# Query projection in bursts of eight heads with paired 64-row TensorE tiles, and shared staging for the output product, in a fused attention-and-MLP kernel

## The chip, the cores and the metric

The kernel runs on one core of a Trainium2 chip. The metric is the device time of one execution in microseconds (us), lower is better. Times are medians of several runs. A single-core run is called fast when it lies within 1.5% of the fastest of the same kernel, and slow otherwise. Kernels are compared only within the same rounds. Engines: PE is the tensor engine (PEld its weight loads), DVE the vector engine, ACT the scalar engine, POOL is GpSimd and SP the engine that issues most transfers.

## The reference

Shapes: 2048 tokens, model width D = 576, 32 query heads over 16 key/value heads of 128, of which the last W = 512 cached positions are used; MLP width 4608. Everything is bf16.

```python
def A(xn, k_cache, v_cache, wq, wo):          # attention, 32 heads
    q = split_heads(xn @ wq)                  # 576 -> 32 x 128
    scores = q @ k^T * 128 ** -0.5            # last 512 positions
    return merge_heads(softmax(scores) @ v) @ wo

def B(xn, w1, w2, w3, w4):
    h = gelu(layernorm(xn) @ w1)
    hs = shift_four_quarters(h) @ w2          # +1, -1, +2, -2 tokens
    x1 = xn + hs
    return x1 + gelu(layernorm(x1) @ w3) @ w4

xn = layernorm(x)
out = x + A(xn) * silu(B(xn))
```

## The kernel before

The attention stage works through four blocks of 512 tokens, 32 heads each; u = 0 to 127 counts the heads. For each head PE does five q matmuls (576 rows padded to 640), four score matmuls and four groups of value matmuls; ACT takes one exponential per score matmul.

```python
qT_pool = pool("qT_pool", 3)
pT_pool = pool("pT_pool", 10)
o_pool = pool("o_pool", 4)
so_pool = pool("so_pool", 1)                  # staging of the wo product
oT_pool = pool("oT_pool", 36)
ps_sc = pool("ps_sc", 3, PSUM)                # score banks
ps_pq = pool("ps_pq", 2, PSUM)                # q banks, also gelu and MLP parts
ps_po = pool("ps_po", 2, PSUM)                # value banks
ps_wo = pool("ps_wo", 1, PSUM)

def stage_q(u):                               # q of ONE head
    psq = ps_pq.tile([P, QB], FP32, name="psq", tag="pq")
    for kc in range(NDC):                     # 5 x 128 rows, the last half zeros
        nc.tensor.matmul(psq, lhsT=w[:, kc, hh*Dh:(hh+1)*Dh], rhs=xT_b[qb % 2][:, kc, :], ...)
    qT = qT_pool.tile([P, QB], BF16, name="qT")
    copy(out=qT, in_=psq)                     # DVE in block 0, ACT after it

def stage_s(u, kc):                           # one score matmul and its exponential
    sc = ps_sc.tile([P, QB], FP32, name="sc", tag="sc")
    nc.tensor.matmul(sc, lhsT=kT[:, g, kc*P:(kc+1)*P], rhs=qT_t[u], ...)
    pT = pT_pool.tile([P, QB], BF16, name="pT")
    nc.scalar.activation(out=pT, in_=sc, func=Exp, scale=SCALE)

def stage_v(u, t0): ...                       # 8 value matmuls into po, DVE writes o
def stage_t(u):                               # o is transposed by DMA, for wo
    o = o_t.pop(u)
    oT = oT_pool.tile([P, TB, P], BF16, name="oT")
    nc.sync.dma_start(out=oT[:], in_=o[:]..., transpose=True)

for u in ...:
    for i in range(4):
        stage_s(u, i)
        if i == 0:
            stage_q(u + 1)                    # one head ahead
            for fn in fill.get(u, []): fn()   # loads, layer norms: placed BY HEAD NUMBER
            continue
        if i < 3: stage_v(u - 1, 2 * (i - 1))
        for fn in cut[i - 1]: fn()            # wo, gelu, k transposes: BY HEAD NUMBER
    stage_t(u - 1)
# ... cut ...
# MLP: weights load once the last oT transpose is issued
with tc.issue_after(last_t[0].ins):
    for i in range(NSL): load_w(i)
load_sx(0)                                    # reads back what wo wrote to DRAM
load_x1(1)
```

What is not a matmul of the head itself (layer norms, their DMA transposes, the small MLP, the wo product of the block before, all weight loads) is pinned to a head number, at so many heads' distance from what needs it.

## Time and profile before

| | before |
|---|---|
| time, median of the first 3 runs | 850.75 us (850.12 to 870.52) |
| profiled span | 847.5 us |
| PE / ACT / DVE busy | 98% / 54% / 50% |
| PE waits of over 2 us each kind | value groups for DVE 2.0, MLP for a fence 2.1 |
| mean granted PE clock | 0.999 |

The page's row of slices cuts the span into 40 equal slices and gives each engine's busy share in tenths. The stage view gives, per stretch of time, the busy time and the number of instructions of PE, PEld, DVE, ACT and POOL, then the granted clock (1 is full speed), the busy share of the 16 DMA engines and GB/s. The order of time gives start, length, engine, line of the kernel, operation, output<-input; in square brackets stands the idle time just before it and what ended it. The lines of before are shown in the prediction, where they are used.

### The profile page before, as it was taken

The page shows a single profiled execution, that of the slowest core. Times are in us where ns is not written, and L with a number is a line of the kernel's source. Part 1 is how long each engine was busy: PE and PEld are TensorE (multiplying, and loading weights), DVE is VectorE, ACT ScalarE, POOL GpSimd, SP SyncE. Part 2 cuts the span into 40 slices and gives each one's busy share as a digit, 9 for nine tenths or more (in the row PEclk, how much of TensorE's full clock was granted, in tenths as well). Part 3 has the DMA queues.
Part 4 walks back from the last instruction along what each step waited for, and adds up shares of the span by engine and source line. Part 5 has one row for each costly group of instructions (what it writes and reads, how often), then busy time and mean ns, then how long its engine had stood idle before and what let it go on. Part 6 is the DMA issues. An engine that isn't in the chain of part 4 may idle for free.

```text
span 847.5 us, 19375 instructions
## 1 busy us (share of the span) xinstructions
PE 826.8 (98%) x7896; PEld 485.0 (57%) x7980; DVE 427.7 (50%) x1351; ACT 460.9 (54%) x825; POOL 76.9 (9%) x134
## 2 busy tenths in 40 slices
PE   8999899999999999999999999999999999999996
PEld 5665555665564565565566565455555555555555
DVE  5778841267751166762154884052247537635324
ACT  5776763598793388784379874132333333334610
POOL 3441200310010111010001100000000000000000
PEclk9999999999999999999999999999999999999999
DMA  7996751473372174363048336992003301310101
GB/s 181 234 234 159 157 97 41 117 125 91 87 136 43 41 130 99 91 126 82 19 82 164 70 79 105 307 342 47 2 2 74 99 2 43 69 64 15 44 15 46
DMA packets 139983, 83.94 MB, mean 99 GB/s; under 512 B 106944, under 2 KB 133248, under 8 KB 139888
## 3 DMA queue, kind: packets, MB, share of 16 engines
q1 hardware_dynamic: 130048, 53.01, 30.6%
q0 software_dynamic: 8448, 28.15, 11.8%
q10 hardware_dynamic: 1392, 1.48, 0.5%
q8 instruction: 64, 1.05, 0.5%
q14 instruction: 31, 0.25, 0.1%
HBM read 49.17 MB, written 9.44 MB: 69 GB/s over the span
## 4 chain that ended last, share of the span: by engine, by line

## 5 line engine op out<-in xcount | busy, mean ns | idle before, releaser
L367 ACT ACTIVATE pT<-sc 128x512 bf16<-128x512 f32 x512 | 290.3, 596 | 103.5 <-PE sc L365 91.4
L365 PE MATMUL sc<-qT,kT 128*128 128x512 bf16 x493 | 175.1, 378 | 1.3 <-DVE qT L355 0.6
L382 PEld LDWEIGHTS <-pT 128*128 128x128 bf16 x2048 | 139.5, 98 | 52.9 <-DVE o L387 2.5
L382 PE MATMUL po<-v_sb,pT 128*128 128x129 bf16 x2048 | 161.4, 220 | 3.2 <-DVE o L387 2.0
L350 PE MATMUL psq<-xT_b,wq_b 128*128 128x512 bf16 x603 | 151.9, 379 | 2.5 <-DMA xT_b<-xn_b 0.4
L386 DVE RECIPROCAL ri_b<-po 128x2 f32<-128x2 f32 x256 | 43.0, 168 | 189.3 <-PE po L382 185.3
L731 PE MATMUL ph<-xT_b,w_s 64*128 64x512 bf16 x976 | 127.1, 376 | 2.3 <-DVE fence L721 2.1
L768 PE MATMUL pm<-w_s,h 64*128 64x512 bf16 x864 | 122.2, 377 | 0.9 <-DVE fence L721 0.9
L406 PE MATMUL pswo<-wo_sb,oT 128*128 128x512 bf16 x497 | 114.2, 379 | 0.8
L387 DVE TENSOR_TENSOR o<-po,ri_b 128x256 bf16<-128x256 f32 x256 | 107.9, 422 | 10.7 <-DMA oT<-o 4.3
L749 ACT ACTIVATE h<-ph 128x512 bf16<-128x512 f32 x67 | 39.4, 597 | 133.9 <-PE ph L731 133.9
L350 PEld LDWEIGHTS <-wq_b 128*128 128x128 bf16 x640 | 62.4, 98 | 74.4 <-issue 2.2
L768 PEld LDWEIGHTS <-h 64*128 64x128 bf16 x1728 | 70.8, 94 | 56.7 <-issue 1.6
L406 PEld LDWEIGHTS <-oT 128*128 128x128 bf16 x1024 | 64.9, 98 | 55.2
L768 PE MATMUL pr<-w_s,h 64*128 64x64 bf16 x864 | 90.2, 189 | 0.2 <-ACT h L749 0.2
L731 PEld LDWEIGHTS <-w_s 64*128 64x128 bf16 x1152 | 57.3, 94 | 51.0 <-issue 2.8
L357 ACT ACTIVATE qT<-psq 128x512 bf16<-128x512 f32 x96 | 57.4, 598 | 28.1 <-PE psq L350 26.7
L747 DVE COPY hx<-ph 128x512 f32<-128x512 f32 x55 | 38.0, 692 | 67.8 <-PE ph L731 67.8
L365 PEld LDWEIGHTS <-kT 128*128 128x128 bf16 x512 | 47.4, 97 | 28.4 <-DVE qT L355 1.2
L227 POOL DMA_DIRECT2D wq_b<-in_A_wq_dram x30 | 23.4, 780 | 314.4 <-PE psq L350 295.4
L721 DVE TENSOR_SCALAR fence<-ph,ph 1x1 f32<-1x1 f32 x61 | 12.6, 206 | 53.9 <-PE ph L731 53.4
L749 ACT ACTIVATE h<-hx 128x512 bf16<-128x512 f32 x55 | 34.6, 630 | 8.5 <-DVE hx L747 7.0
(114 smaller groups left out, 641.3 us busy)
## 6 DMA issues: line engine op xcount, KB each, us to landing
wq_b<-in_A_wq_dram POOLq DMA_DIRECT2D x30, 512.0 KB, 5.3
w_s<-in_B_w_dram SPq DMA_DIRECT2D x9, 576.0 KB, 7.0
wo_sb<-in_A_wo_dram POOLq DMA_DIRECT2D x8, 576.0 KB, 5.0
w_s<-in_B_w_dram SPq DMA_DIRECT2D x9, 512.0 KB, 7.9
x_dram<-x SPq DMA_DIRECT2D x4, 576.0 KB, 3.5
x<-x_dram SPq DMA_DIRECT2D x4, 576.0 KB, 5.1
s_b<-s_dram SPq DMA_DIRECT2D x4, 576.0 KB, 5.4
x_b<-in_A_x_dram SPq DMA_DIRECT2D x4, 576.0 KB, 6.6
```

The source lines that it names most:

```text
L350: nc.tensor.matmul(psq[:, :], lhsT=w[:, kc, hh * Dh:(hh + 1) * Dh], rhs=xT_b[qb % 2][:, kc, :], start=(kc == 0), stop=(kc == NDC - 1))
L357: nc.scalar.activation(out=qT[:, :], in_=psq[:, :], func=ACT.Copy)
L365: nc.tensor.matmul(sc[:, :], lhsT=kT[:, g, kc * P:(kc + 1) * P], rhs=qT_t[u][:, :], start=True, stop=True)
L367: nc.scalar.activation(out=pT[:, :], in_=sc[:, :], func=ACT.Exp, scale=SCALE)
L382: nc.tensor.matmul(po[:, j, :], lhsT=pTs[kc][:, tt * P:(tt + 1) * P], rhs=v_sb[:, g, kc, 0:Dh + 1], start=(kc == 0), stop=(kc == KCH - 1))
L386: nc.vector.reciprocal(out=ri, in_=po[:, :, Dh])
L387: nc.vector.tensor_tensor(out=o[:, t0:t0 + 2, :], in0=po[:, :, 0:Dh], in1=ri.unsqueeze(2).to_broadcast([P, 2, Dh]), op=ALU.mult)
L406: nc.tensor.matmul(ps, lhsT=oT_t[qb * Hq + h][:, tt, :], rhs=wo_sb[:, h, lo:hi], start=(h == 0), stop=(h == Hq - 1))
L731: nc.tensor.matmul(ps[i][:, :], lhsT=lhsT, rhs=xT[half, kc, :], start=first, stop=last, skip_group_check=True)
L747: nc.vector.tensor_copy(out=src[:, :], in_=ps[i][:, :])
L749: nc.scalar.activation(out=h3[:, :], in_=src[:, :], func=ACT.Gelu_apprx_tanh)
L768: nc.tensor.matmul(out, lhsT=h3_t[b, fc][half, tt * P:(tt + 1) * P], rhs=w4_s[fc // WS][half, fc % WS, lo:hi], start=key not in started, s ...
```

## The change

The intent is to save the zero padding of the q contraction. Two heads share PE as two tiles of 64 rows: both heads' 576 rows are nine half steps each, and two half steps run at once, one in the upper and one in the lower rows. First five pairs (F), then the halves swap banks for four more (S), with a one-element DVE fence between. q is now made for eight heads at a time, in the two q and the two value banks. To make room, the staging of the wo product shares existing buffers, and the o pool goes from 4 to 3.

```diff
-        qT_pool = pool("qT_pool", 3)
+        qT_pool = pool("qT_pool", 8)
-        o_pool = pool("o_pool", 4)
+        o_pool = pool("o_pool", 3)
-        so_pool = pool("so_pool", 1)
...
-            eng.dma_start(out=w[0:DR, NF, :], in_=A_wq[NF * P:D, c0:c0 + 4 * Dh])
+            for half in (LO, HI):
+                eng.dma_start(out=w[half, NF, :], in_=A_wq[NF * P:D, c0:c0 + 4 * Dh])
...
+        def stage_qs(u0, n):
+            pend = None
+            for i in range(n // 2 + 1):
+                nxt = None
+                if i < n // 2:
+                    psp, tag = ((ps_pq, "pq"), (ps_po, "po"))[(n // 2 - 1 - i) % 2]
+                    nxt = (u0 + 2 * i, [psp.tile([P, QB], FP32, name="psq", tag=tag) for _ in range(2)])
+                    q_half(xT, *nxt, [(kc, ((0, LO), (1, HI))) for kc in range(NDC)], True)      # F
+                    ... one-element DVE fence on both banks
+                if pend:
+                    u, ps = pend
+                    q_half(xT, u, ps, [(kc, ((1, LO), (0, HI))) for kc in range(NF)], False)    # S
+                    nc.scalar.activation(out=qT_t[u][:, :], in_=ps[0][:, :], func=ACT.Copy)
+                    nc.vector.tensor_copy(out=qT_t[u + 1][:, :], in_=ps[1][:, :])
+                pend = nxt
...
-                    so_t[qb] = so_pool.tile([P, TB, D], BF16, name="s_out")
+                    so_t[qb] = w1_sb[:, 0:TB, :] if qb == NB - 1 else x1_pool.tile([P, TB, D], BF16, name="x1")
...
-                        if u + 1 < U:
-                            stage_q(u + 1)
+                if u == 4:
+                    stage_qs(4, 4)
+                elif u % 8 == 0 and 0 < u < U:
+                    stage_qs(u, 8)
```

The loads of the q weights move with it, and the head's extra PE work is cut into four parts instead of three.

More of the change, by code (lines that the diff above doesn't have):

```diff
@@ L76 @@
     PAD = 2
+    LO, HI = slice(0, P // 2), slice(P // 2, P)
     VW = Dh + 2
@@ L274 @@
             x_t[0].append(xt)
-        for w in xn_b + [xnn_b]:
-            nc.gpsimd.memset(w[:, :, D:], 0.0)
-        for w in wq_b:
-            nc.gpsimd.memset(w[DR:, NF, :], 0.0)
+        nc.gpsimd.memset(xnn_b[:, :, D:], 0.0)
         with tc.manual_schedule(engines={SP}):
@@ L314, in ln1_steps @@
             xn_t[b] = xn_b[b % 2]
-            return layernorm_steps(small, [xn_b[b % 2][:, tt, 0:D] for tt in range(TB)], [x[:] for x in x_t.pop(b)],
-                                   rsqrt_newton if b else rsqrt_table)
+            return layernorm_steps(small, [xn_b[b % 2][:, tt, :] for tt in range(TB)], [x[:] for x in x_t.pop(b)],
+                                   rsqrt_newton if b else rsqrt_table, twice=True)
         def transpose_tile(dstT, src, tt):
@@ L342 @@
         qT_t, pT_t, o_t, oT_t = {}, {}, {}, {}
-        def stage_q(u):
-            qb, h = divmod(u, Hq)
-            w = wq_b[(u // 4) % NWQ]
-            hh = h % 4
-            psq = ps_pq.tile([P, QB], FP32, name="psq", tag="pq")
-            for kc in range(NDC):
-                nc.tensor.matmul(psq[:, :], lhsT=w[:, kc, hh * Dh:(hh + 1) * Dh], rhs=xT_b[qb % 2][:, kc, :],
-                                 start=(kc == 0), stop=(kc == NDC - 1))
-            qT = qT_pool.tile([P, QB], BF16, name="qT")
-            with tc.high_priority(offset=HP):
-                if qb == 0:
-                    nc.vector.tensor_copy(out=qT[:, :], in_=psq[:, :])
-                else:
-                    nc.scalar.activation(out=qT[:, :], in_=psq[:, :], func=ACT.Copy)
-            qT_t[u] = qT
+        def stage_qs(u0, n):
+            qb = u0 // Hq
+            xT = xT_b[qb % 2]
+            pend = None
[5 more added lines that the diff above has]
+                    q_half(xT, *nxt, [(kc, ((0, LO), (1, HI))) for kc in range(NDC)], True)
+                    f = small.tile([1, 1], FP32, name="fence")
+                    with tc.high_priority(offset=2 * HP):
+                        nc.vector.tensor_scalar(out=f[:, :], in0=nxt[1][0][0:1, 0:1], scalar1=nxt[1][1][0:1, 0:1],
+                                                scalar2=None, op0=ALU.add)
+                if pend:
+                    u, ps = pend
+                    q_half(xT, u, ps, [(kc, ((1, LO), (0, HI))) for kc in range(NF)], False)
+                    for k in range(2):
+                        qT_t[u + k] = qT_pool.tile([P, QB], BF16, name="qT")
+                    with tc.high_priority(offset=HP):
+                        nc.scalar.activation(out=qT_t[u][:, :], in_=ps[0][:, :], func=ACT.Copy)
+                        nc.vector.tensor_copy(out=qT_t[u + 1][:, :], in_=ps[1][:, :])
+                pend = nxt
@@ L360, in stage_s, with q_half @@
+        def q_half(xT, u, ps, steps, first):
+            w = wq_b[(u // 4) % NWQ]
+            for kc, halves in steps:
+                for k, half in halves:
+                    hh = (u + k) % 4
+                    nc.tensor.matmul(ps[k][:, :], lhsT=w[half, kc, hh * Dh:(hh + 1) * Dh], rhs=xT[half, kc, :],
+                                     start=(first and kc == 0), stop=(not first and kc == NF - 1), skip_group_check=True)
         def stage_s(u, kc):
@@ L424, in rem @@
                     (nc.scalar if qb == NB - 1 else nc.sync).dma_start(out=rows(s_dram, qb * TB, TB),
-                                                                       in_=so_t.pop(qb)[:])
+                                                                       in_=so_t.pop(qb)[:, :, :])
             for tt in range(TB):
@@ L614 @@
                 pe_late.append((2 * g - 3, g))
-        for j in range(2, NB * 8):
-            at(4 * (j - 1) - 1, lambda j=j: load_wq(j))
+        at(1, lambda: load_wq(2))
+        for j in range(3, NB * 8):
+            at(4 * (j - 2) + (1 if j % 2 else 5) if j > 3 else 4, lambda j=j: load_wq(j))
         for b in range(NB):
@@ L637 @@
             tr1_first()
-            stage_q(0)
+            stage_qs(0, 4)
             for fn in prep_k(1):
@@ L643 @@
                 n = len(atoms)
-                cut = [atoms[0:n // 3], atoms[n // 3:2 * n // 3], atoms[2 * n // 3:]]
+                if u == 4:
+                    stage_qs(4, 4)
+                elif u % 8 == 0 and 0 < u < U:
+                    stage_qs(u, 8)
                 for i in range(4):
@@ L648 @@
                     if i == 0:
-                        if u + 1 < U:
-                            stage_q(u + 1)
                         for fn in fill.get(u, []):
                             fn()
-                        continue
-                    if i < 3 and 0 <= u - 1 < U:
+                    elif i < 3 and 0 <= u - 1 < U:
                         stage_v(u - 1, 2 * (i - 1))
-                    for fn in cut[i - 1]:
+                    for fn in atoms[n * i // 4:n * (i + 1) // 4]:
                         fn()
@@ L708 @@
         h3_t = {}
-        LO, HI = slice(0, P // 2), slice(P // 2, P)
         fence_pool = pool("fence", 2)
```

## The prediction

> **What bounds the kernel now.** I read the page first: the busy shares and the row of slices, which say which engine is full and when.
>
> ```profile
> PE 826.8 (98%) x7896; PEld 485.0 (57%) x7980; DVE 427.7 (50%) x1351; ACT 460.9 (54%) x825; POOL 76.9 (9%) x134
> ...
> PE   8999899999999999999999999999999999999996
> ...
> ACT  5776763598793388784379874132333333334610
> ```
>
> PE is full from end to end. ACT averages 54%, but in slices 3 to 25 (the attention stage, about 10 to 553 us) it swings between 3 and 9 tenths: the average hides stretches in which ACT is nearly full as well. So next I took the stage totals, and one stretch in which a head has no extra PE work. Columns: length, then busy us (instructions) of PE, PEld, DVE, ACT, POOL, then granted clock, DMA share and GB/s.
>
> ```profile
> 10.40:120.20 109.80, 106.07 (x898) 66.33 (x915) 83.29 (x269) 80.78 (x145) 30.90 (x52) 1.00 0.86 179
> 120.20:253.90 133.70, 132.64 (x1104) 79.19 (x1122) 65.10 (x225) 92.17 (x171) 17.40 (x30) 1.00 0.44 96
> 253.90:388.20 134.30, 132.86 (x1105) 79.23 (x1123) 65.21 (x226) 92.23 (x171) 12.99 (x21) 1.00 0.44 91
> 388.20:522.50 134.30, 133.02 (x1116) 79.42 (x1134) 68.21 (x231) 88.75 (x163) 7.92 (x12) 1.00 0.40 81
> 299.67:316.93 17.26, 17.10 (x150) 10.87 (x151) 12.52 (x51) 15.96 (x31) 2.16 (x4) 1.00 0.74 151
> ```
>
> The last row is six heads without extra work: PE is busy 17.10 of 17.26 us and ACT 15.96. PE decides, but ACT is 7% behind it. The order of time shows one such head:
>
> ```profile
> 300.78 1.24 PE L350 MATMUL psq<-xT_b,wq_b 128*128 128x512 bf16 x5
> ...
> 301.86 0.38 PE L365 MATMUL sc<-qT,kT 128*128 128x512 bf16 x1
> ...
> 302.06 0.60 ACT L357 ACTIVATE qT<-psq 128x512 bf16<-128x512 f32 x1 [0.21 <-PE psq L350]
> ...
> 302.07 0.63 PE L382 MATMUL po<-v_sb,pT 128*128 128x129 bf16 x8
> ...
> 302.54 0.38 PE L365 MATMUL sc<-qT,kT 128*128 128x512 bf16 x1
> ...
> 302.55 2.17 ACT L367 ACTIVATE pT<-sc 128x512 bf16<-128x512 f32 x4
> ...
> 304.74 0.38 PE L365 MATMUL sc<-qT,kT 128*128 128x512 bf16 x1
> ```
>
> Starts give the true pitches: five q matmuls take 301.86-300.78 = 1.08 us (0.216 each), a score matmul 0.21, eight value matmuls 0.47, and the head 304.74-301.86 = 2.88 us. That is 4x0.216 + 2x0.47 + 1.08. The four exponentials are 2.17 us back to back (0.543 each), and the q copy is 0.60: 2.77 us of ACT per head. A copy starts 0.20 us after the matmul stream it reads.
>
> **What the Trainium skill says.** "TensorE: Matmul & The Clock Gate", Back-to-back issue gap: N/2.4+2.5 ns, 216 ns for 512 columns; the trace's 0.216 agrees. "TensorEngine Tiling (Array Packing)", Key Properties: tiles work independently, but a change of tiling mode drains the engine. The MLP stage already uses pairs of 64-row tiles:
>
> ```profile
> 549.94 3.90 PE L406 MATMUL pswr<-wo_sb,oT 128*128 128x64 bf16 x128
> 553.77 1.04 PE L731 MATMUL ph<-xT_b,w_s 64*128 64x512 bf16 x8
> ...
> 554.65 0.38 PE L731 MATMUL ph<-xT_b,w3r_s 64*128 64x512 bf16 x2
> ```
>
> Eight half matmuls advance by 0.88 us, so a pair costs 0.22, the same as one full matmul; and no gap is seen at the change of mode, so I charge nothing for drains. Same page, PSUM Bottleneck: tiling speeds up TensorE "but not PSUM evacuation". I take that as the point here. "PSUM — Partial Sum Buffer", on bank collisions: two row tiles may not write one bank at a time. Hence the added fence before the halves swap banks; no run here shows a collision.
>
> **The change part by part.**
> *Removed: padding.* A head's contraction of 576 ran as five 128-row steps, the last half zeros. Two heads now take 5 pairs, then 4 swapped pairs: 9x0.216 = 1.94 us, not 2.16. Over 64 pairs of heads that is 13.8 us less PE work, all on the engine that is full. This is the intended gain, -1.6%.
> *Moved: q out of the heads into bursts of eight.* The other PE work of a head is 2.88-1.08 = 1.80 us, but its exponentials need 2.17. The three score banks let PE run only three exponentials ahead. So heads without extra work become ACT-bound. The loop from the end of one head's last exponential through two value groups and two scores to the next last exponential is 0.06+1.36+0.20+0.54, again 2.2 us. I use 2.2. In a burst PE does 7.8 us of q, while ACT has four copies (2.4 us) and at most three leftover exponentials (1.6 us), then starves. Before, q filled exactly that slack.
> *Added: waits inside a burst.* The built PE order is F0 F1 S0 F2 S1 F3 S2 S3 (F a pair's first ten half matmuls, S its last eight). Pairs alternate between the two q banks and the two value banks, so F2 waits for the copies of pair 0 right after S0 and F3 for those of pair 1 right after S1. Each wait is 0.20 lag + 0.69 (the DVE copy) + 0.06 (the restart lag seen after an exponential) = 0.95 us; two per burst. F0 also needs the bank of the value group just issued: 0.2+0.17+0.42+0.06 after its end, less one score matmul, some 0.6 us. A burst of eight then delays the exponentials by about 7.8+1.9+0.6-0.3 (PE briefly ahead afterwards) = 10.0 us. Fences should hide behind the next F.
> *Cost per block.* Before, a block of 32 heads is 4 wo heads at 9.78, one at 6.6, 8 with one five-matmul group at 3.96, one at 4.75 and 18 plain at 2.88: 134 us, as measured. After: 4x8.70 + 5.5 + 8x2.88 + 3.7 + 18x2.2 = 106.6, plus four bursts of 10.0: 146.6. That is +12.6 each in blocks 1 and 2. Block 3 has 13 plain heads, more second-MLP groups and three bursts: 108.7+30 = 138.7, +4.4. Block 0 up to the start of wo: first score at about 15.3 (four heads projected before it), 33 heads x 2.2 = 72.6, five gelu groups +3.5, a half burst +4, four bursts +40 (one serves block 1 already), and +2.5 because at head 24 the built DVE order puts a layer norm's steps between fences and copies. Sum 137.9 against 120.2: +17.7.
> *Rest.* ACT loses 32 q copies, worth 19 us of busy time, but not where it binds: bursts leave it idle. The shared output buffers, the fewer o buffers and the doubled 64-row loads cost nothing that I can see: the wo output buffers are written with work around them, and the DMA share is 0.4 in blocks 1 to 3. The MLP stage (553.8 to the end, 293.7 us) is untouched.
> Sum: 17.7+12.6+12.6+4.4 = +47; I shade this to +43, since some of the block 0 terms overlap.
>
> **Rivals.**
> *The padding gain stands.* If PE stayed full, the time would be 850.75-13.8 = 837. For it: PE is the bound at 98%, and 64-row pairs run at full pitch in the MLP. Against it: it needs ACT to have slack in plain heads, where it needs 2.17 us against 1.80, and the bursts' eviction waits to vanish.
> *Only ACT starvation, no eviction waits.* If the copies overlapped more than I think, bursts cost about 8.0: 15.5 bursts x 2 = 31 us less, so about 863. Against it: the waits on both copies stand in the built order ahead of F2 and F3, and each copy lasts 0.6 or 0.69 us.
> *Weights late.* Both q weight buffers are used by one burst, so the next eight heads' weights load only after it (5.3 us from issue to landing, with 17 us or more available). Blocks 1 to 3 should hide it; block 0, with a DMA share of 0.86, may not, for +3 to +10 us, toward 900.
> *Tile switches cost.* 33 mode changes at some tenths of a us would add 5 to 10 us.
>
> **Range and chances.** Centre 850.75+43 = 894 us. Burst cost is the widest term: 1.5 us either way on 15.5 bursts is 23 us; with block 0's loads above it, 870 to 914. Faster by over 2% needs a gain beyond the whole padding term, so 0.03. Within 2% (up to 868) needs nearly all waits inside bursts to be hidden: 0.10. Slower: 0.87.
>
> **What would show it.** In the changed profile, plain heads should repeat every 2.2 us with ACT back to back and PE waiting for score banks; bursts should last about 9.7 us, with two idle gaps near 0.9 us ended by a q copy, ACT nearly idle after its leftover exponentials. PE's share should fall to about 92%, its q busy time should hardly matter, and the MLP stage should still take about 294 us. I am wrong if plain heads stay near 2.9 us, if bursts take 7.8, or if the loss lies in the MLP stage or in waits for q weights.

## The result and the profile after

The changed kernel takes **985.83 us** (median of 5 runs, 984.46 to 995.0) against 852.02 us (5 runs) for the kernel before on the same chip. The ratio of fast runs is 1.159 (95%: 1.151 to 1.166). A ratio here is the mean time of one kernel's fast runs over that of the other's of the same rounds, so not quite the ratio of the medians quoted. The direction was right; the size, +134 us for +43, was not. The profile below is of the slowest of the five runs (995.0 us, 9 above the median), so its stages together show some 9 us more than the medians do.

The page of the changed kernel, shares and slices:

```profile
PE 871.1 (88%) x8492; PEld 499.8 (50%) x8492; DVE 460.0 (46%) x1463; ACT 438.2 (44%) x793; POOL 90.4 (9%) x160
...
PE   7865986999888899897799998897899999999997
...
ACT  5461843336557334663633566520233333332620
...
PEclk9986988999999899899899999999899999999999
```

PE, full in every slice before, now has holes all through the attention stage (slices 1 to 28), deepest in the first ten. PE's busy time even rose by 44 us although its work shrank: the clock row is below 9 where the holes are, and there the same matmul takes longer (some 24 us, estimated below; the rest is not taken apart). ACT is not fuller than before. So nothing new is the bound over the whole span; PE waits.

The stage view of the changed kernel, cut at the same events as the stages of before (first q, the four starts of a wo product, its end):

```profile
11.80:178.20 166.40, 124.70 (x1091) 74.01 (x1090) 81.96 (x277) 83.21 (x157) 34.98 (x60) 0.89 0.67 120
178.20:340.15 161.95, 142.54 (x1251) 82.06 (x1250) 76.75 (x262) 83.52 (x155) 21.35 (x38) 0.97 0.36 83
340.15:507.03 166.88, 144.86 (x1251) 83.90 (x1250) 77.12 (x263) 83.47 (x155) 20.46 (x35) 0.95 0.34 81
507.03:656.50 149.47, 134.69 (x1214) 78.45 (x1213) 76.66 (x258) 80.36 (x148) 7.51 (x13) 0.99 0.32 71
...
688.00:993.20 305.20, 285.12 (x3349) 158.24 (x3348) 138.06 (x370) 100.63 (x170) 0.00 (x0) 0.98 0.28 80
```

| stage | before | predicted | changed | changed less predicted |
|---|---|---|---|---|
| block 0 | 109.8 | 127.5 | 166.4 | +38.9 |
| block 1 | 133.7 | 146.6 | 162.0 | +15.4 |
| block 2 | 134.3 | 146.6 | 166.9 | +20.3 |
| block 3 | 134.3 | 138.7 | 149.5 | +10.8 |
| last wo product | 31.3 | 31.3 | 31.5 | +0.2 |
| MLP | 293.7 | 293.7 | 305.2 | +11.5 |

(The prediction's block 0 ends at 137.9, so 137.9-10.4 = 127.5.) Every stage but the wo tail is over. Block 0 is the least steady: with the attention code unchanged it took 161.8 and 158.3 us in two later runs (`e9_order`, `e2_order`). The waits of PE say on what; columns: total us, times, longest:

```profile
PE po L398 <- DVE o L403: 32.1, 8, 9.5
PE psq L373 <- ACT qT L364: 20.2, 29, 0.7
PE ph L747 <- DMA w_s<-in_B_w_dram: 11.1, 1, 11.1
PE psx L521 <- DVE hs L510: 9.2, 3, 4.0
PE ph L470 <- DMA xnnT<-xnn_b: 7.2, 2, 4.1
```

Only the second line, the wait inside a burst for a q copy, is one that the prediction counted. Here is one burst, in order of time, on PE, ACT and DVE alone:

```profile
225.18 0.37 PE L373 MATMUL psq<-xT_b,wq_b 64*128 64x512 bf16 x1 [0.20 <-DVE ri_b L402]
225.85 3.19 PE L373 MATMUL psq<-xT_b,wq_b 64*128 64x512 bf16 x27 [0.29 <-DVE o L403]
...
229.07 0.60 ACT L364 ACTIVATE qT<-psq 128x512 bf16<-128x512 f32 x1 [3.47 <-PE psq L373]
...
229.72 2.12 PE L373 MATMUL psq<-xT_b,wq_b 64*128 64x512 bf16 x18 [0.68 <-ACT qT L364]
...
232.54 3.02 PE L373 MATMUL psq<-xT_b,wq_b 64*128 64x512 bf16 x26 [0.70 <-ACT qT L364]
```

The burst runs from 225.18 to the first score matmul at 235.50: 10.3 us, with two stops of 0.7 us that a q copy ends and 0.5 us at the start for the value banks. ACT idles 3.47 us in its midst. After it the plain heads follow: the trace has 20 exponentials in 10.27 us from 236.10 on, so 0.513 each and 2.05 us per head. All of that is close to the prediction (9.7 us, two gaps near 0.9, 2.2 us). What was not predicted lies elsewhere. The first line of the list, in order of time, in block 0, with a later value group for comparison in the last line:

```profile
65.04 8.35 SPq L317 DMA_TRANSPOSE xnnT<-xnn_b  x1
71.58 0.43 DVE L403 TENSOR_TENSOR o<-po,ri_b 128x256 bf16<-128x256 f32 x1 [8.12 <-DMA oT<-o]
72.06 1.05 PE L398 MATMUL po<-v_sb,pT 128*128 128x129 bf16 x8 [7.31 <-DVE o L403]
...
236.63 0.63 PE L398 MATMUL po<-v_sb,pT 128*128 128x129 bf16 x8
```

PE waits for the DVE scaling of a head's output, but DVE waits 8.12 us itself, for a free o buffer: the DMA transpose of an earlier head's output has not landed. DVE waits 41.6 us in all for that. And after the 7.31 us stop the same eight value matmuls take 1.05 instead of 0.63. The Trainium skill says so in "TensorE: Matmul & The Clock Gate", section Why this matters for your kernels: no idle gaps of PE over about 3 us, or the clock falls back to half. The trace agrees in the main: block 0, which has most such stops, was granted 0.89, and the kernel before, which has none, 1.00. Stage views around single stops, first across those of 7.31 and 9.53 us, then after one of 2.48 us (its end is at 322.91) and after one of 3.12 us (its end is at 253.17):

```profile
67.10:90.90 23.80, 9.31 (x55) 6.27 (x57) 4.03 (x14) 3.37 (x6) 1.06 (x2) 0.50 0.91 155
323.00:329.80 6.80, 5.54 (x33) 3.53 (x34) 1.49 (x6) 1.19 (x2) 0.00 (x0) 0.50 0.53 106
253.20:263.00 9.80, 8.42 (x72) 4.02 (x73) 5.49 (x15) 3.62 (x6) 0.41 (x1) 1.00 0.19 39
```

So near 3 us the limit is not sharp here: 2.48 us brought the half clock, 3.12 us did not. The 0.7 us stops inside a burst did not either (1.00 over the burst shown above). The profiled run has ten stretches at 0.50, 78 us together, in which PE was busy for 48 us; at full speed that work would take about half, so the slow clock cost PE some 24 us (an estimate from these stage views).

The start of the MLP, loads as SP issues them. First the changed kernel, then the kernel before:

```profile
688.05 0.36 SPq L717 DMA_DIRECT2D s_b<-s_dram  x1
...
689.63 1.30 SPq L702 DMA_DIRECT2D w_s<-in_B_w_dram  x1
...
699.07 1.46 PE L747 MATMUL ph<-xT_b,w_s 64*128 64x512 bf16 x6 [11.05 <-DMA w_s<-in_B_w_dram]
```

```profile
525.83 0.46 SPq L685 DMA_DIRECT2D w_s<-in_B_w_dram  x1
```

Before, the first MLP weights were asked for at 525.83, some 28 us ahead of their use. Now the read-back of the wo product stands ahead of them in the same queue; it can only go when that product is done (688.05), so the weights start at 689.63 and PE stands 11.05 us.

### The profile page after: what moved, and what is told of

The parts are those of the page before. It is cut to its first block, busy times and chain, and to the rows that moved or that the text cites.

```text
span 993.2 us, 20694 instructions
## 1 busy us (share of the span) xinstructions
PE 871.1 (88%) x8492; PEld 499.8 (50%) x8492; DVE 460.0 (46%) x1463; ACT 438.2 (44%) x793; POOL 90.4 (9%) x160
## 4 chain that ended last, share of the span: by engine, by line
## 5 line engine op out<-in xcount | busy, mean ns | idle before, releaser
L383 ACT ACTIVATE pT<-sc 128x512 bf16<-128x512 f32 x512 | 277.3, 603 | 150.6 <-PE sc L381 145.3
L398 PE MATMUL po<-v_sb,pT 128*128 128x129 bf16 x2048 | 175.2, 225 | 34.0 <-DVE o L403 32.1
L398 PEld LDWEIGHTS <-pT 128*128 128x128 bf16 x2048 | 143.1, 100 | 99.5 <-DVE o L403 39.3
L381 PE MATMUL sc<-qT,kT 128*128 128x512 bf16 x512 | 179.1, 388 | 1.5 <-ACT pT L383 1.0
L373 PE MATMUL psq<-xT_b,wq_b 64*128 64x512 bf16 x1152 | 147.0, 395 | 35.2 <-ACT qT L364 20.2
L747 PE MATMUL ph<-xT_b,w_s 64*128 64x512 bf16 x976 | 127.9, 378 | 13.1 <-DMA w_s<-in_B_w_dram 11.1
L403 DVE TENSOR_TENSOR o<-po,ri_b 128x256 bf16<-128x256 f32 x256 | 107.3, 421 | 47.1 <-DMA oT<-o 41.6
L373 PEld LDWEIGHTS <-wq_b 64*128 64x128 bf16 x1152 | 72.4, 98 | 108.1 <-issue 56.8
L422 PE MATMUL pswo<-wo_sb,oT 128*128 128x512 bf16 x512 | 118.4, 379 | 4.2 <-ACT x L432 4.2
L364 ACT ACTIVATE qT<-psq 128x512 bf16<-128x512 f32 x64 | 38.2, 597 | 140.4 <-PE psq L373 140.4
L747 PEld LDWEIGHTS <-w_s 64*128 64x128 bf16 x1152 | 57.6, 94 | 62.6 <-DMA w_s<-in_B_w_dram 11.2
L763 DVE COPY hx<-ph 128x512 f32<-128x512 f32 x55 | 38.0, 691 | 67.5 <-PE ph L747 67.5
L365 DVE CAST qT<-psq 128x512 bf16<-128x512 f32 x64 | 44.2, 691 | 29.6 <-PE psq L373 29.6
L356 DVE TENSOR_SCALAR fence<-psq 1x1 f32<-1x1 f32 x64 | 13.4, 209 | 72.6 <-PE psq L373 72.6
```

What stands on the lines that cost most here:

```text
L364: nc.scalar.activation(out=qT_t[u][:, :], in_=ps[0][:, :], func=ACT.Copy)
L365: nc.vector.tensor_copy(out=qT_t[u + 1][:, :], in_=ps[1][:, :])
L373: nc.tensor.matmul(ps[k][:, :], lhsT=w[half, kc, hh * Dh:(hh + 1) * Dh], rhs=xT[half, kc, :], start=(first and kc == 0), stop=(not first a ...
L381: nc.tensor.matmul(sc[:, :], lhsT=kT[:, g, kc * P:(kc + 1) * P], rhs=qT_t[u][:, :], start=True, stop=True)
L383: nc.scalar.activation(out=pT[:, :], in_=sc[:, :], func=ACT.Exp, scale=SCALE)
L398: nc.tensor.matmul(po[:, j, :], lhsT=pTs[kc][:, tt * P:(tt + 1) * P], rhs=v_sb[:, g, kc, 0:Dh + 1], start=(kc == 0), stop=(kc == KCH - 1))
```

## The experiments

Three suspects came out of the profile: too few o buffers, the order of the first MLP loads, and the q weight loads, which now come two together after each burst and might crowd the transposes. The rival to all three was that the burst itself, or the 64-row tiles in it, cost more than the trace shows.

### First call: each suspect alone, then all

The kernel before spread from 851 to 869 us. The intervals given are of fast runs alone.

**Four o buffers again**, with one exponential buffer fewer to make room:

```diff
-        pT_pool = pool("pT_pool", 10)
-        o_pool = pool("o_pool", 3)
+        pT_pool = pool("pT_pool", 9)
+        o_pool = pool("o_pool", 4)
```

> The changed kernel with four o buffers again instead of three (one exponential buffer fewer, nine for ten, to make room). Theory buffers: the three o buffers are why the normalization waits for the transposing DMA (41.6 us in the changed kernel, with PE behind it for some 32 us and at half clock after the long stops); with four the wait falls under 12 us and the time by 25 to 40 us, to about 945 to 960. Rival loads: the transposes are held up by the two q weight loads issued back to back after each burst; a fourth buffer buys one head (about 2 us) for each of some eight stops, so only 10 to 18 us, to 968 to 976.

Measured: 974.03 us, 1.137 times before (1.126 to 1.148). DVE's waits for transposes fell from 41.6 to 15.7 us and PE's from 32.1 to 7.5, but the time fell by only 12 us, which is the rival's range (968 to 976): PE then waited 10.2 us for q weights and 6.2 for xT transposes, which it had not before (2.9 and none). The buffer matters, but a wait that goes is largely replaced by another.

**MLP weights queued first:**

```diff
-        load_sx(0)
-        load_x1(1)
+        with tc.issue_after(last_w.ins):
+            load_sx(0)
+            load_x1(1)
```

> The changed kernel with the first loads of the MLP stage in the order of the kernel before: MLP weights first, then the attention results and x. Theory order: PE's stop of 11.05 us at the start of the MLP stage comes from the weights queued behind a load that waits for the end of wo; the MLP stage falls from 305 to about 294 us, the time by 11 to 12 us, to about 974, and the attention stage stays. Rival: the weights wait for the shared output buffers' store; then the stop stays and the time with it (985).

Measured: 1009.16 us (1.182), slower. This was a mistake of mine, not a test: the edit put the load of x1 behind all the weights too, and PE then stood 32.7 us for the layer norm that needs it (`PE ph L747 <- DVE hx L763: 32.9, 2, 32.7`). It gave one useful number: its attention stage, whose code is the same, ended at 645.1 instead of 656.5 us, so that stage varies by some 10 us from run to run.

**The two q-weight loads three heads apart,** each gated by an exponential of that head:

```diff
-            at(4 * (j - 2) + (1 if j % 2 else 5) if j > 3 else 4, lambda j=j: load_wq(j))
+            uj = 4 * (j - 2) + (0 if j % 2 else 1) if j > 3 else 5
+            at(uj, lambda j=j, uj=uj: late(pT_t[uj][0][0:1, 0:1], lambda: load_wq(j)))
```

> The changed kernel with the two q weight loads after each burst three heads apart, each gated by an exponential of its head, instead of back to back; three o buffers. Theory loads: transposes land in time again, the normalization's wait on them falls from 41.6 to under 15 us and the time by 25 to 40 us, to 945 to 960. Rival buffers: with three o buffers any transpose over some 4 us stops the value products; the wait falls by less than a third, the time by under 12 us (over 973).

Measured: 999.32 us (1.166; 1.155 to 1.177), no gain; DVE's waits for transposes were 49.6 us. That the pairs of q loads crowd the transposes falls as the main cause.

**All three edits together:**

> All three together: four o buffers (nine exponential buffers), MLP loads in the order of before, q weight loads spaced. If the bursts' own cost was predicted rightly, what is left is the predicted 894 us, give or take 12: bursts of 10.4 us, plain heads of 2.1 us, an MLP stage of 294 us. If it stays over 925, bursts cost more than their eviction waits and ACT's starvation.

Measured: 1005.0 us (1.173). It holds the 33 us stop of the mistaken order, so without it about 972. Even so it is far from the predicted 894: the three suspects together do not hold the missing time.

### Second call: the order mended, and the burst taken apart

**Only the read-back behind the weights**, the x1 load stays in front:

```diff
-        load_sx(0)
+        with tc.issue_after(last_w.ins):
+            load_sx(0)
         load_x1(1)
```

> The changed kernel with only the loads of the attention results and x moved behind the MLP weights; the load of the second block's x1 stays ahead of the weights, as in the kernel before (the earlier try pushed it back too, and PE waited 32.7 us for it). Theory order: PE's stop of 11 us at the start of the MLP stage goes, that stage takes 294 us, the time falls by about 11 us against the changed kernel's 985. Rival: the stop moves to another load and the stage stays at 305.

Measured: 978.8 us (1.148; 1.141 to 1.155); the before took 851.13. PE's 11 us stop for the first MLP weights is gone from the list of waits, and the MLP stage takes 292.8 us (before 293.7), as expected. By medians the time falls by about 7 us; the two intervals overlap, so the stage, not the total, is the evidence.

**Bursts of eight, but q by five padded 128-row matmuls** in the two q banks: no tiles, no fences, no swap.

```diff
-            for i in range(n // 2 + 1): ... F and S halves in four banks, fence
+            for u in range(u0, u0 + n):
+                ps = ps_pq.tile([P, QB], FP32, name="psq", tag="pq")
+                for kc in range(NDC):
+                    nc.tensor.matmul(ps[:, :], lhsT=w[:, kc, hh * Dh:(hh + 1) * Dh], rhs=xT[:, kc, :], ...)
+                ... copy by DVE (odd u) or ACT (even u)
```

> The changed kernel with its bursts of eight, but each head's q projected by five full 128-row matmuls in the two q banks, copies by ACT and DVE in turn: no 64-row tiles, fences or mode changes. Theory burst: what costs is that q is gathered (ACT starves in the burst, binds outside it, and work scheduled by the count of heads comes late); a burst takes 8.6 us instead of 10.4, so 15.5 x 1.8 = 28 us less and the time about 957. Rival tiles: fences, mode changes and eviction waits of the 64-row tiles are the loss; then under 900.

Measured: 953.66 us (1.117; 1.111 to 1.124), as expected. With the padding back and next to no eviction wait (1.9 us in the whole run) the kernel is 32 us faster than the changed one, but still 12% slower than before. So the tiles are not most of the loss. What is left is not the bursts' own cost alone: this run still has three o buffers, the 11 us stop at the MLP and the late work, which later runs take away.

**64-row tiles for a pair of heads at a time, no bursts** (two q banks; four o buffers; the order mended; layer norm two heads earlier):

```diff
-                if u == 4:
-                    stage_qs(4, 4)
-                elif u % 8 == 0 and 0 < u < U:
-                    stage_qs(u, 8)
+                qu = u + 2 if u % 2 == 0 and u + 2 < U else None
+                    if i == 0 and qu: q_first(qu)          # F after the first score matmul
+                    if i == 1 and qu: q_second(qu)         # S one step later
```

> 64-row tiles without bursts: for each pair of heads the ten first half matmuls after one head's first score, the eight swapped ones after its first value group, in the two q banks; four o buffers, MLP loads in the order of before, layer norm of the next block two heads earlier. Theory burst: ACT stays fed, PE carries 1.94 us plus four mode changes of 0.12 us per pair instead of 2.16, so about +0.27 us x 64 = 17 us against the kernel before: 867 (855 to 885). Rival tiles: over 930.

Measured: 907.49 us (1.064; 1.058 to 1.071), a miss by 40 us. The clock is 0.999, so spreading q does keep PE warm, but a pair of plain heads takes 6.2 to 6.6 us where two heads took 5.76 before. In the order of time a plain pair has four changes of mode, each of some 0.1 us, and a stop of 0.16 us after the swapped halves: 0.46 us more per pair, or 29 us for 64 pairs (an estimate). The expectation had 0.27 us. The rest of the 56 us stands mostly in the list of PE's waits:

```profile
PE psq L367 <- DVE fence L350: 12.4, 16, 1.2
PE psq L367 <- DVE g_x L479: 9.4, 11, 1.2
```

These 22 us fall where a pair meets gelu groups: it needs both q banks at once, and the same two banks also serve those groups. F waits for their copies, and S for the fence, which DVE reaches late. I had counted the halves' matmuls and the changes of mode, but no such wait.

**Bursts of four** (F0 F1 S0 S1, each pair in its own banks, so no copy is waited for inside the burst; four o buffers; order mended):

```diff
-                elif u % 8 == 0 and 0 < u < U:
-                    stage_qs(u, 8)
+                if u % 4 == 0 and 0 < u < U:
+                    stage_qs(u, 4)
```

> The changed kernel with bursts of four heads instead of eight: the order F0 F1 S0 S1 has no wait for an eviction, one weight buffer is used per burst; four o buffers, MLP loads in the order of before. Theory burst: the eviction waits (20 us) go, a part of the transpose waits and slow-clock time (30 us) and the MLP stop (11 us) go, ACT's starvation stays: about 925 (905 to 945). Rival evictions: if the waits inside bursts and what follows from them were all, it comes to 850 to 880.

Measured: 918.86 us (1.078; 1.071 to 1.084), a hit. Half-size bursts without eviction waits cost much less, at a clock of 0.989; of the 67 us to the changed kernel some 19 are the o buffers and the order, by the runs of these alone.

### Third call: parts of the change alone on the kernel before, and the distances

What stayed unexplained in the changed kernel were waits such as `psx <- hs` (9.2 us) and `ph <- xnnT` (7.2 us): work placed at a number of heads before its use. A plain head now lasts 2.05 us instead of 2.88, so the same number of heads is less time. That was the new theory. The parts that I had called free were also tried alone.

**The kernel before with three o buffers** (five rounds):

```diff
-        o_pool = pool("o_pool", 4)
+        o_pool = pool("o_pool", 3)
```

> The kernel before with three o buffers instead of four, nothing else. The prediction said that fewer o buffers cost nothing to be seen. In the kernel before transposes land in 3.2 us (median) and a head takes 2.88 us, so three buffers leave some 6 us: within 0 to 6 us of before (under 0.7%). Rival: the buffer count alone explains the transpose waits of the changed kernel; then over 20 us slower.

Measured: 855.54 against 855.45 us; ratio 1.0014 (0.9985 to 1.0044): the same. Three buffers are enough where heads come evenly.

**The kernel before with the shared wo staging** (five rounds):

```diff
-                    so_t[qb] = so_pool.tile([P, TB, D], BF16, name="s_out")
+                    so_t[qb] = w1_sb[:, 0:TB, :] if qb == NB - 1 else x1_pool.tile([P, TB, D], BF16, name="x1")
```

> The kernel before with only the wo results staged in the shared buffers. Theory order: this part alone turns the order of the first MLP loads round (the built order shows it), so PE stops for about 11 us at the start of the MLP stage and the time is 858 to 864; the attention stage is unchanged. Rival: the MLP stop belongs to the bursts; then 851.

Measured: 867.35 us, 1.0154 (1.0098 to 1.0211), a little over the expected range. One line in PE's waits of this run is new:

```profile
PE ph L730 <- DMA w_s<-in_B_w_dram: 11.3, 1, 11.3
```

It is the stop of the changed kernel. So a part that touches no attention work costs 12 us by itself, because sharing the buffers alters the order in which the scheduler issues the first loads of the next stage.

**The changed kernel with wider distances** (layer norm 2 and its transposes three heads earlier, the small MLP's second product one or two later, layer norm 1 two earlier, a head's extra PE work only after its first score; plus four o buffers and the mended order):

```diff
-            later(base + 7, lambda b=b: ln2_steps(b), 3)
+            later(base + 4, lambda b=b: ln2_steps(b), 3)
-                at(base + 10 + tt, lambda b=b, tt=tt: tr2(b, tt))
+                at(base + 7 + tt, lambda b=b, tt=tt: tr2(b, tt))
-                o2 = base + (28 if bb == b else 23 if b == NB - 1 else 21)
+                o2 = base + (28 if bb == b else 24 if b == NB - 1 else 23)
-                u1 = base + (24 if b else 20)
+                u1 = base + (22 if b else 20)
-                    for fn in atoms[n * i // 4:n * (i + 1) // 4]:
+                    for fn in atoms[n * (i - 1) // 3:n * i // 3] if i else []:
```

> The changed kernel with its bursts of eight 64-row pairs, with the MLP loads' order mended, four o buffers, and the work that is placed by counting heads given more of them: the second layer norm three heads earlier, the shift and second matmul of the MLP's first layer one or two heads later, the next block's layer norm two heads earlier, wo and MLP matmuls only after a value group. Theory distance: heads of 2.1 us instead of 2.9 brought this work late; PE's waits for hs, xnnT, xT, psx and the wo bank (some 35 us with the slow clock after them) go, and the time is 920 to 945. Rival: the waits move elsewhere; over 960.

Measured: 937.18 us (1.098; 1.093 to 1.104), a hit, 42 us less than the run with the mended order alone. The four o buffers were worth 12 us when tried alone, so the distances and the regrouped extra work are worth some 30 if the two add up; that pair was not run without them. Its stages (blocks 1 to 3, and the MLP):

```profile
163.80:316.20 152.40, 142.22 (x1254) 80.18 (x1252) 81.07 (x261) 82.11 (x156) 21.32 (x38) 0.97 0.39 88
316.20:466.20 150.00, 139.82 (x1253) 79.60 (x1251) 81.04 (x262) 82.03 (x156) 20.57 (x35) 0.99 0.40 91
466.20:607.90 141.70, 132.10 (x1206) 77.77 (x1204) 77.73 (x255) 78.43 (x146) 7.33 (x12) 1.00 0.33 73
...
639.40:932.40 293.00, 283.82 (x3349) 158.06 (x3348) 137.99 (x370) 100.61 (x170) 0.00 (x0) 1.00 0.28 77
```

Blocks 1 to 3 take 152.4, 150.0 and 141.7 us where the prediction has 146.6, 146.6 and 138.7, and the MLP 293.0 for 293.7. With most side effects gone, the predicted burst model holds there to 3 to 6 us. Block 0 stayed at 152.0 for 127.5.

**The same, with q by 128-row matmuls in the bursts:**

> The same, but q in bursts of eight by 128-row matmuls. What is left is the pure price of gathering q: ACT starves in a burst and binds in plain heads. From plain heads of 2.1 us and bursts of 8.9: 106.6 + 4 x 8.9 = 142 us per block against 134, in all about 30 us, so 880 (870 to 905). If it is under 860, gathering costs nothing and the eviction waits were all; over 915, something else is still late.

Measured: 900.25 us (1.054; 1.049 to 1.059), in the range. From 937 to 900 is 37 us: that is what the 64-row tiles with their shared banks cost inside bursts of eight, though they save 13.8 us of matmul time. Blocks 1 and 2 of this run take 139.4 us each at full clock, only 5 more than before:

```profile
156.30:295.70 139.40, 138.07 (x1125) 79.15 (x1123) 77.69 (x245) 82.76 (x155) 17.20 (x30) 1.00 0.39 92
```

But its block 0 takes 144.5 (before 109.8), with 22.3 us of PE waits for outputs whose transposes are late, all of them in that block.

### Fourth call: what is special in block 0

Block 0 carries the loads of all keys, values and output weights, with a DMA share of 0.69 in the run with wide distances. Either these transfers crowd the transposes and the q weights, or those are late because of what stands before them in program order. To tell the two apart, loads were taken away: 7 of 8 output-weight loads and 12 of 16 value loads, about 5.6 MB, while all matmuls stay (they reuse the loaded part, so these results are wrong, though they still passed the comparison with the reference).

```diff
-        v_sb = res.tile([P, Hkv, KCH, VW], BF16, name="v_sb")
+        v_sb = res.tile([P, 4, KCH, VW], BF16, name="v_sb")
-        wo_sb = pool("a_wo", 1).tile([P, Hq, D], BF16, name="wo_sb")
+        wo_sb = pool("a_wo", 1).tile([P, 4, D], BF16, name="wo_sb")
-                at(2 * g - 8, lambda g=g: load_v(g // 2))
-        for i in range(8):
+        for i in range(1):
             at(4 + 3 * i, lambda i=i: late(..., lambda: load_wo(i)))
```

**On the run with wide distances:**

> A wrong result on purpose: e12 with only the first four value groups and the first four heads' output weights loaded (24 transfers on the software queue fewer than 128 KB to 576 KB each: 7 of 8 output-weight loads, 12 value loads, about 5.6 MB less in block 0); the matmuls keep their number, size and order. Theory A (block 0's 24 us above the prediction come from transfers that crowd each other: q weights 7.8 us and output transposes 6.2 us late, and the clock that falls after them): block 0 goes from 152.0 to about 130 to 138 us, the two waits vanish, the clock there rises from 0.91 to above 0.96, and the time falls from 937 to about 915 to 923. Theory B (the transposes and weights are late because of what stands before them in program order, not for bandwidth): block 0 stays at 147 or more and the time within 6 us of 937.

Measured: 917.99 us (1.075; 1.069 to 1.081), 19 us less, in the expected range. Block 0 in the run with wide distances, then in this one:

```profile
11.80:163.80 152.00, 125.52 (x1099) 71.72 (x1099) 83.07 (x279) 83.96 (x160) 34.78 (x60) 0.91 0.69 132
```

```profile
12.00:147.60 135.60, 121.85 (x1099) 70.07 (x1099) 83.09 (x279) 83.73 (x160) 20.99 (x36) 0.96 0.49 105
```

With the same 1099 PE instructions, block 0 falls from 152.0 to 135.6 us, the clock rises from 0.91 to 0.96, and both waits (q weights 7.8, o 6.2) are gone from PE's list. For the q weights this does not settle crowding against order: the loads taken away (19 transfers; the 24 of the expectation is too many) stood before them among GpSimd's own, and in the run with wide distances GpSimd waited 3.0 us for a key and a value load before it issued their last parts. For the transposes the next pair of runs is cleaner, as no q weight was late in it.

**On the run with 128-row bursts:**

> A wrong result on purpose: the same lightening on e13 (128-row bursts). Theory A: the 22.3 us for late output transposes in block 0 vanish, block 0 goes from 144.5 to about 122 to 128, the time from 900 to about 878 to 884. Theory B: time within 6 us of 900.

Measured: 874.91 us (1.026; 1.022 to 1.030), 25 us less, somewhat better than expected; block 0 is 121.6 us at full clock.

**Control, on the kernel before:**

> A wrong result on purpose, as a control: the same lightening on the kernel before, where PE waits for no transfer in block 0. Both theories: 850 to 857, block 0 within 2 us of 109.8. If it gains more than 5 us, the lightening itself changes something else and e14 and e15 do not count at their full size.

Measured: 849.17 us against 853.49 for the kernel before (ratio 0.994; 0.992 to 0.996); block 0 takes 109.2. The lightening alone is worth some 4 us by medians and 4 to 7 by the ratio's interval on a kernel without bursts, though its block 0 is as before; that is at the limit of 5 us that I had set. So of the 19 and 25 us some 15 and 21, or a few less, come from block 0's traffic meeting the bursts.

**With twelve o buffers as well,** in the freed space, and ten exponential buffers:

> A wrong result on purpose: e14 with twelve o buffers and ten exponential buffers in the space that the lightening freed. Theory A: within 4 us of e14, as no transpose is late enough to hold a buffer any more. Theory B: 6 us or more below e14, as late transposes still hold the buffers in block 0 and more buffers outlast them.

Measured: 915.94 us (1.0745; 1.070 to 1.079), the same ratio as with four. Once the transfers are not crowded, no transpose is late enough to hold a buffer. "DMA: Bandwidth & Descriptors" of the Trainium skill, section Issuing engines are not separate DMA queues, says that transfers started by different engines run on the same 16 DMA engines and interleave. These runs agree: the loads taken away were issued by GpSimd, and the transposes that became punctual by SP.

## Why the prediction was right or wrong

**Right.**
- *ACT-bound plain heads and starved bursts.* Plain heads repeat every 2.05 us (2.2 predicted), a burst takes 10.3 (7.8+1.9+0.6 = 10.3 in the prediction's terms), with two stops of 0.7 us ended by a q copy, for 0.95 predicted. Padding saved did not reach the time, as argued against the first rival.
- *PE's share* fell to 88% (about 92% predicted), and at head 24 PE waited 3.0 us for a DVE copy held up by a layer norm (2.5 predicted).
- The rival *Weights late* came true, and only in block 0: 2.9 us in the changed kernel, 7.8 where the other waits had been taken out.
- *Tile switches*: 34 changes of mode at 0.10 to 0.12 us, read from the gap between the pitch's end and the next start, make 3 to 4 us. Small, but I had charged nothing.

**Wrong.** The sum +47 missed 87 us. (The range was also mis-summed: 894 with 23 either way is 871 to 917, not 870 to 914.) The step that failed is the paragraph *Rest*, which called the parts outside the bursts free, and with it the sum per block, which left out how work is timed and what the loads of block 0 do. In the order in which the runs removed it:
1. *"The MLP stage (553.8 to the end, 293.7 us) is untouched."* It took 305.2: the first weights were issued behind the read-back of the wo product. Mending the order gave 7 us, the staging alone on the kernel before cost 12. The built instruction order of SP, to be seen before any run, showed this.
2. *"The shared output buffers, the fewer o buffers and the doubled 64-row loads cost nothing that I can see."* For the o buffers this is true alone (ratio 1.0014) and false together with late transposes: 12 us.
3. *A term that the cost per block lacks: the distances.* I let plain heads shrink from 2.88 to 2.2 us and did not ask what else was timed in heads. Layer norms, their transposes and the small MLP's copies came too late. Widening the distances took some 30 us out.
4. *Block 0, "+17.7".* It counted bursts and ACT as in the other blocks and dismissed the DMA share, quoting the 0.4 of blocks 1 to 3 and giving the 0.86 of block 0 only to the weights. Removing loads took 15 us (19 less the control's 4) out of the kernel with wide distances.
5. *The clock.* No term held it. It was granted 0.89 in block 0 of the changed kernel and 1.00 before. It adds to every long stop, and is part of points 1 to 4. No run takes it away alone; by the estimate above it is some 24 us of the profiled run.

What then remains is 918.0 less 853.5 = 64 us, or 69 against the lightened kernel before (849.2): 17 to 22 more than the sum of +47. By stage it is 8 us in block 0 and 3 to 6 in each other block. The trace of that run has one line to explain it:

```profile
PE psq L373 <- DVE qT L365: 8.2, 3, 2.9
```

In one burst each of blocks 0, 1 and 2, PE stops for a q copy that stands behind a layer norm on DVE. The prediction had this once, with 2.5 us. In the changed kernel it happens once too (3.0 us); moving that layer norm two heads earlier, in the run with wide distances, most likely brought it into the bursts of blocks 1 and 2. After these stops the clock is 0.50 for 23 us, with PE busy for 20, so another 10 us (an estimate). Together that is about 16 us beyond the 2.5, most of the remainder.

The parts (7 for the order, 12 and 30 for buffers and distances, 15 to 19 for block 0's traffic, 17 to 22 left) add up to about 86 of the 87 us. That is no test: the 30 and the rest are themselves differences between runs, across calls whose medians for the kernel before differ by up to 4 us. Of the rivals, *only ACT starvation* (863) came nearest to a kernel that was run: 128-row bursts with the side effects and the traffic removed took 874.91, and with the padding put back the rival's figure is 863+14 = 877. The tiles add 43 us to that (918.0 less 874.9), more than the 31 that the same rival gave for the eviction waits; the three stops behind a layer norm are a part of it, as the 128-row run has none.

Left open: the clock's share by experiment; the run-to-run spread of some 10 us in the changed kernel's attention stage; how much of the q weights' lateness is order in GpSimd's queue; and whether the bursts do better with the layer norm kept out of them. No version with a right result beat the kernel before.

## What to carry to other kernels

A schedule whose parts are placed by iteration count is a schedule in time only while iterations keep their length: before shortening the common iteration, list what is placed by its number and convert each distance to microseconds, before and after. Work taken out of an evenly loaded loop and gathered in bursts saves nothing if it was what filled the waits for a second engine that is nearly full, and a stop of 2.5 us or more that it causes may cost twice, in the stop and in a slower clock after it. A buffer that changes its pool "for free" can turn round the order of transfers in a queue; compare the built order of each queue, not only the allocation.

## What the Trainium skill lacked or had wrong

- "TensorEngine Tiling (Array Packing)", Key Properties, says that a change of tiling mode drains the engine, but gives no size: here a change from 128-row to 64-row matmuls or back cost 0.10 to 0.12 us, little in bursts (34 changes), but some 26 us (an estimate) where 64 pairs were spread out, with four changes each.
- The same page, PSUM Bottleneck, advises both ScalarE and VectorE for eviction; it doesn't say what a pair of row tiles costs when its two banks must both be free: each pair that met a busy bank stopped PE for 0.7 us although both engines copied, and 64-row bursts were 37 us slower than padded 128-row bursts.
- "DMA: Bandwidth & Descriptors" has bandwidths for DMA transposes, but no latency for small ones beside other loads: a 128x512 transpose of one head's output took 2.4 us from issue to landing at best and 22.6 at worst in the changed kernel.
- "TensorE: Matmul & The Clock Gate" was right for long stops: after one of 7.31 us the same eight matmuls took 1.05 us, not 0.63. Its limit of about 3 us was not sharp: a stop of 2.48 us brought 6.8 us of half clock, stops of 2.88 and 3.12 us none. The page gives no odds for stops of this size; in the changed kernel ten stretches at half clock, 78 us together, cost some 24 us (an estimate).
